# Gated-convolution FFN after pooled attention: VectorE's convolution in units of its middle weight, and three steps moved between engines

## The chip, the cores and the metric

The kernel runs on one core of a Trainium2 chip. The metric is device time in microseconds (us), the median of the runs; a run of the kernel before took 216.84 to 217.48 us. PE is TensorE (matmul), PEld its weight loads, DVE is VectorE, ACT is ScalarE, POOL is GpSimd, SP is the queue that issues most transfers.

## The reference

Inputs are q, k, v of shape (8, 8, 576, 64) in float32 (batch, heads, sequence, head size), and the FFN's weights.

```python
k_p = k.reshape(B, H, Sp, 8, D).mean(axis=3)          # Sp = 72
v_p = v.reshape(B, H, Sp, 8, D).mean(axis=3)
scores = (1 / sqrt(D)) * q @ k_p^T
attn = softmax(scores - max(scores))
x = (attn @ v_p), heads side by side                   # (8, 576, 512)

h = maximum(x @ w_in, 0)                               # (8, 576, 1024)
conv_out[s] = conv_w[0]*h[s-1] + conv_w[1]*h[s] + conv_w[2]*h[s+1]   # per column of h, zero outside
gate = 1 / (1 + exp(-conv_out))
out = (h * gate) @ w_out                               # (8, 576, 512) float32
```

## The kernel before

The eight batches are taken in four groups of two. Attention works on tiles of 128 query rows: ten tiles in group 0 and nine in each later group, 37 in all. For a tile, PE makes the scores of all heads in PSUM (`att_scores`), VectorE takes the maximum of each head (`att_max`, L608) and, from group 1 on, subtracts it (`att_shift`, L620; in group 0 PE adds it), ScalarE takes the exponential (`att_exp`, L646), PE or a transposing DMA turns the result (`att_turn`, `att_send`), PE multiplies by the pooled values (`att_values`, L682), and VectorE divides by the sum of each head: a reciprocal of 8 columns (L695) and a multiplication of 512 columns (L697), both in `att_divide`. The result x is turned into `xT`, by PE in groups 0 and 1 (`att_turn_out`, L714, and a copy), by a DMA on SP's queue in groups 2 and 3 (`att_out`).

The FFN runs per batch, with the hidden columns on the partitions: eight blocks of 128 columns (`fb` 0 to 7), four blocks being a quarter `(b, f4)`, so sixteen quarters in all. PE projects in (`ffn_in`, L727), ScalarE applies Relu into `hT` (`ffn_relu`, L736) with scale 0.5. Then comes the convolution over the sequence, in one of two ways:

- On PE (`ffn_conv`, L889): 64x64 blocks of diagonal matrices `dw`, two blocks `fb` at a time, so that the upper and lower halves of every odd block come out exchanged. ScalarE's tanh (`ffn_tanh`, L914) writes even blocks to `gT` and odd ones to a side buffer `tg`; VectorE adds 1 (`ffn_gate`: L925 for the even blocks, twice L927 for the odd ones, which also puts the halves right) and multiplies by `hT` (`ffn_times`, L935). Ten quarters go this way.
- On VectorE, for the quarters in `Graph.TAPS`, six before: ScalarE makes the middle tap (`ffn_tap`, L862, Identity with a scale per partition) into a float32 buffer of the ring `tg`, which has three, VectorE adds the two side taps (L864), ScalarE takes the tanh (`ffn_tap_tanh`, L869), VectorE adds 1 and multiplies by `hT` (`ffn_tap_gate`, L875 and L876).

The sequence lies in `hT` in nine pieces; for batches in `Graph.WRAP` GpSimd copies 63 columns to each end (`ffn_wrap`, L811, L812), so that each tap is one contiguous read. Since Relu halves h and the weights `convw` are doubled, `tanh(conv / 2) + 1` times `hT` is the gated value.

PE projects out per tile of 128 rows (`ffn_out`, L943), ScalarE or VectorE copies the result (`ffn_copy`, L954), and SP's or ScalarE's queue stores it (`ffn_store`). A tile of the last group needs the gates of all its batches' quarters.

The order of all work is written out: `Graph.ORDER` lists every operation (its index twice, plus one if it takes the second of two engines), `FORMS` the shapes of some matmul groups and `PLACES` the PSUM banks and buffers. Each engine works through its part of that order; a negative entry is a filler matmul. `add(...)` states for each operation its engines, a cost that a planner used, and what it follows.

Of the kernel before, what the change touches and what calls it, by code (L numbers as in the profile page):

```python
# [33 lines left out]
class Graph:  # L34
# [24 lines left out]
    WRAP = (4, 5, 6, 7)  # L59
    TAPS = ((4, 1), (5, 0), (5, 1), (6, 0), (6, 1), (7, 0))  # L60
    ACC = 2
    WRAPS = 2
    CROSS = ()
# [3 lines left out]
    SHIFT_PE = ((0, 0), (0, 1), (0, 2), (0, 3), (0, 4), (0, 5), (0, 6), (0, 7), (0, 8), (0, 9))  # L67
    TURN_DMA = 2
    BANKS = 8
    ORDER = (  # L70
# [107 lines left out]
def kernel(  # L178
# [13 lines left out]
    POOL = 8  # L192
# [1226 lines left out]
```

## Time and profile before

| | |
|---|---|
| runs | 216.84, 217.14, 217.48 us; median 217.14 us |
| the profiled execution | span 216.5 us from the first to the last instruction; no other time of it is given |
| instructions | 6617 |
| mean granted TensorE clock | 0.992 |
| data read, written in HBM | 32.52 MB, 9.44 MB |

A row of the groups gives the line, engine, operation, output and inputs with partitions x columns and type, the count, then busy us in all and the mean ns of one, then the idle time of the engine just before them and what ended it. A row of the stretches gives from:to, the length, and the busy us of PE, PEld, VectorE, ScalarE and GpSimd with their instruction counts, then the granted clock, the busy share of the DMA engines and GB/s. A piece of the chain gives its start, its length and what ran; a row of the timeline the same with shapes, `xN` for a run of N, and in brackets the idle time before it.

### The profile page before, as it was taken

What the parts mean: (1) busy time and instruction counts of PE and PEld (TensorE: products, weight loads), DVE (VectorE), ACT (ScalarE), POOL (GpSimd) and SP (SyncE); (2) the same over time, 40 slices, a digit from 0 to 9 for tenths busy, and PEclk for the clock granted to TensorE, in tenths of its full rate; (3) what the DMA queues carried; (4) which work ended last, traced back from release to release, by engine and by line L of the source; (5) the groups of instructions that cost most, each with busy time, mean ns of one, the idle gap of its engine ahead of it and who ended that gap; (6) DMA issues with size and microseconds to landing.
All of it is one profiled execution on the core that took longest, in us unless ns stands there. A gap on an engine that the chain in (4) does not pass through costs nothing.

```text
span 216.5 us, 6617 instructions
## 1 busy us (share of the span) xinstructions
PE 201.9 (93%) x2753; PEld 137.0 (63%) x2753; DVE 193.2 (89%) x334; ACT 162.7 (75%) x278; POOL 41.5 (19%) x78
## 2 busy tenths in 40 slices
PE   7599999969999999999999899989999999999992
PEld 3557778855788776766776675665656666654451
DVE  7598989999999999999999799999899999998621
ACT  2548885896998887787497594878979999997420
POOL 8644330050052101000000030002201210370000
PEclk9799999999999999999999999999999999999999
DMA  6999999999999999969687634576347745602685
GB/s 210 227 207 209 206 207 208 210 205 206 207 205 206 154 153 179 158 164 165 131 111 100 136 74 89 58 156 148 78 104 153 158 100 123 145 0 51 169 242 171
DMA packets 48833, 33.46 MB, mean 155 GB/s; under 512 B 28300, under 2 KB 43812, under 8 KB 48804
## 3 DMA queue, kind: packets, MB, share of 16 engines
q0 software_dynamic: 15216, 15.40, 43.5%
q1 hardware_dynamic: 32512, 16.13, 36.6%
q10 hardware_dynamic: 1076, 1.52, 2.5%
q8 instruction: 21, 0.34, 0.7%
q14 instruction: 8, 0.07, 0.1%
HBM read 32.52 MB, written 9.44 MB: 194 GB/s over the span
## 4 chain that ended last, share of the span: by engine, by line
PE 45%; DVE 34%; issue 6%; ACT 6%; DMA 5%; SPq 2%; DVEq 0%
PE psum L943 20%; PE psum L727 16%; DVE negm L608 7%; DVE x L697 6%; DVE sd L620 4%; DVE gT L935 4%; DMA hT<-in_k_dram 3%; DVE v L486 3%; DVE gT L927 3%; PE psum L889 2%; DMA out_dram<-osb 2%; DVE r L695 2%; PE psum L682 2%; ACT e L646 2%; DVE gT L925 1%
## 5 line engine op out<-in xcount | busy, mean ns | idle before, releaser
L727 PE MATMUL psum<-xT,w_in_sb 128*128 128x288 bf16 x512 | 74.1, 286 | 2.2 <-DMA xT<-x 1.1
L943 PE MATMUL psum<-w_out_sb,gT 128*128 128x512 bf16 (+1 forms) x296 | 69.5, 374 | 0.7 <-DVE gT L935 0.6
L727 PEld LDWEIGHTS <-w_in_sb 128*128 128x128 bf16 x512 | 47.9, 98 | 19.1 <-issue 2.0
L736 ACT ACTIVATE hT<-psum 128x576 bf16<-128x576 f32 x64 | 40.3, 650 | 14.0 <-PE psum L727 13.4
L943 PEld LDWEIGHTS <-gT 128*128 128x128 bf16 x296 | 27.3, 98 | 26.5 <-issue 0.9
L864 DVE SCALAR_TENSOR_TENSOR tg<-hT,convw,tg 128x576 f32<-128x576 bf16 x48 | 37.6, 815 | 0.5
L608 DVE TENSOR_REDUCE negm<-psum 128x8 f32<-128x576 f32 (+2 forms) x37 | 27.5, 752 | 2.3 <-PE psum L582 1.6
L697 DVE TENSOR_TENSOR x<-psum,r 128x512 bf16<-128x512 f32 (+1 forms) x37 | 25.6, 691 | 1.4
L811 POOL COPY hT<-hT 128x126 bf16<-128x126 bf16 x16 | 7.5, 467 | 97.6 <-ACT hT L736 80.1
L620 DVE TENSOR_TENSOR sd<-psum,negm 128x576 f32<-128x576 f32 x27 | 20.2, 753 | 0.5
L682 PE MATMUL psum<-vm,eT 128*128 128x130 bf16 (+5 forms) x240 | 18.9, 222 | 1.1 <-DVE x L697 0.7
L646 ACT ACTIVATE e<-sd 128x576 bf16<-128x576 f32 x27 | 18.2, 685 | 1.3 <-DVE sd L620 1.1
L954 ACT COPY osb<-psum 128x512 f32<-128x512 f32 x27 | 15.7, 585 | 4.4 <-PE psum L943 4.2
L889 PE MATMUL psum<-hT,dw 64*64 64x288 bf16 (+2 forms) x608 | 18.7, 261 | 0.1
L682 PEld LDWEIGHTS <-eT 128*128 128x128 bf16 (+1 forms) x240 | 15.3, 100 | 5.4 <-DMA eT<-e 1.2
L862 ACT ACTIVATE tg<-hT,convw 128x576 f32<-128x576 bf16 x24 | 18.1, 772 | 0.1
L889 PEld LDWEIGHTS <-dw 64*64 64x64 bf16 x608 | 14.8, 107 | 4.6 <-issue 3.7
L869 ACT ACTIVATE gT<-tg 128x576 bf16<-128x576 f32 x24 | 16.3, 683 | 0.7 <-DVE tg L864 0.5
L914 ACT ACTIVATE gT<-psum 128x576 bf16<-128x576 f32 x20 | 12.9, 651 | 3.9 <-PE psum L889 2.7
L914 ACT ACTIVATE tg<-psum 128x576 bf16<-128x576 f32 x20 | 13.0, 652 | 2.6 <-PE psum L889 1.4
L935 DVE TENSOR_TENSOR gT<-gT,hT 128x2304 bf16<-128x2304 bf16 x10 | 13.5, 1352 | 0.1
L486 DVE TENSOR_TENSOR v<-v 128x1280 bf16<-128x1280 bf16 (+2 forms) x24 | 13.0, 540 | 0.2
(84 smaller groups left out, 234.2 us busy)
## 6 DMA issues: line engine op xcount, KB each, us to landing
out_dram<-osb SPq DMA_DIRECT2D x54, 128.0 KB, 2.4
v<-in_v_dram POOLq DMA_DIRECT2D x8, 512.0 KB, 13.1
qp<-in_q_dram POOLq DMA_DIRECT2D x7, 576.0 KB, 14.4
kk<-in_k_dram POOLq DMA_DIRECT2D x3, 1152.0 KB, 14.6
out_dram<-qp ACTq DMA_DIRECT2D x10, 128.0 KB, 2.7
hT<-in_k_dram SPq DMA_DIRECT2D x2, 576.0 KB, 5.0
w_in_sb<-in_moe_w_in_dram POOLq DMA_DIRECT2D x2, 512.0 KB, 14.2
w_out_sb<-in_moe_w_out_dram POOLq DMA_DIRECT2D x1, 1024.0 KB, 24.7
```

Of the source, the lines that this page charges most:

```text
L608: nc.vector.tensor_reduce(out=a["m"][0:rows], in_=a["s"][0:rows, :, 0:2 * KW].rearrange("p a (h s) -> p a h s", s=Sp), axis=AX.X, op=OP.ma ...
L620: nc.vector.tensor_tensor(out=a["d"][0:rows], in0=a["s"][0:rows, :, 0:2 * KW].rearrange("p a (h s) -> p a h s", s=Sp), in1=a["m"][0:rows]. ...
L646: nc.scalar.activation(out=dst, in_=src, func=ACT.Exp, scale=1.0 / (POOL * 8.0),)
L682: nc.tensor.matmul(out=a["o"][lo:hi, h // 4, (h % 4) * (D + 1):(h % 4 + x1 - x0) * (D + 1)], lhsT=a["eT"][:, j, lo:hi], rhs=buf("vm", b)[: ...
L697: nc.vector.tensor_tensor(out=a["x"][0:rows].rearrange("p (a h d) -> p a h d", a=2, d=D), in0=ov[:, :, :, 0:D], in1=r[0:rows].unsqueeze(3) ...
L727: nc.tensor.matmul(out=banks(ps)[:, j, 0:SC], lhsT=w_in_block(dc, fb), rhs=buf("xT", g)[:, dc, i * S + j * SC:i * S + (j + 1) * SC], start ...
L736: nc.scalar.activation(out=h_of(b)[:, fb].rearrange("p (a s) -> p a s", a=2), in_=banks(ps)[:, :, 0:SC], func=ACT.Relu, scale=0.5,)
L864: nc.vector.scalar_tensor_tensor(out=acc, in0=h, scalar=w, in1=acc, op0=OP.mult, op1=OP.add)
L889: nc.tensor.matmul(out=banks(pss[r ^ c])[c * D:(c + 1) * D, j, lo:hi], lhsT=dw[r * D:(r + 1) * D, tap * n_fb + fb, :], rhs=hT[r * D:(r + 1 ...
L914: nc.scalar.activation(out=t.rearrange("p (a s) -> p a s", a=2), in_=banks(ps)[:, :, 0:SC], func=ACT.Tanh, scale=0.5,)
L935: nc.vector.tensor_tensor(out=gate, in0=gate, in1=h_of(b)[:, four], op=OP.mult)
L943: nc.tensor.matmul(out=bank(ps)[0:rows, columns], lhsT=buf("gT", g)[:, fb, t * P:t * P + rows], rhs=w_out_sb[:, fb, columns], start=(fb == 0),
```

## The change

1. **Taps.** VectorE's convolution is taken in units of the middle weight: `ratio[:, 0]` and `ratio[:, 2]` are the side weights divided by the middle one, `ratio[:, 1]` is half the middle weight, built once by seven small VectorE instructions (a weight of nearly zero is replaced by a tiny one). The first tap reads `hT` twice (`h * ratio + middle h`), the second adds to the buffer, and ScalarE's tanh takes the middle weight as its scale per partition. ScalarE's middle tap goes.
2. **Two more quarters off PE.** (4, 0) and (3, 1) join `TAPS`; batch 3 joins `WRAP`.
3. **Gates cross on ScalarE.** For every quarter left on PE, ScalarE writes an odd block's tanh in two instructions of 64 partitions, each into the exchanged half of `gT`; VectorE then adds 1 in one instruction of 2304 columns in place of three.
4. **Late sigmoids.** In the quarters of batches 6 and 7, ScalarE takes the sigmoid itself (Relu then with scale 1.0), and VectorE's "+1" goes. A sigmoid waits until every exponential has started; the instruction order has one further table load on ScalarE, between the 56th and the 57th Relu.
5. **Split division.** The reciprocal (`att_invert`) and the multiplication (`att_divide`) are operations of their own; the multiplication may go to ScalarE as eight instructions of 64 columns with a scale per partition. The new order puts 9 of 37 there.
6. **The pooling's 1/8 and the scores' 1/8** move from the exponential's scale into the pooling matrix and a scaled identity `ident_k`.
7. `ORDER`, `FORMS` and `PLACES` are new. A form of the exponential by head (`by_head`) is added and not used (`EIGHT = ()`). Output buffers of the last group now follow the turned queries of all of batches 4 to 7.

The changed program's instruction order has, against that of before: on VectorE 64 taps for 48, 12 gate additions for 36, 28 divisions for 37, eight small instructions more in the preparation; on ScalarE 72 division pieces, 48 tanh or sigmoid instructions behind PE's convolution for 40, 32 behind the taps for 24, no middle taps for 24; on PE 480 convolution matmuls for 608 and 26 fillers for 17; on GpSimd 40 edge copies for 32.

```diff
-    WRAP = (4, 5, 6, 7)
-    TAPS = ((4, 1), (5, 0), (5, 1), (6, 0), (6, 1), (7, 0))
+    WRAP = (3, 4, 5, 6, 7)
+    TAPS = ((4, 0), (4, 1), (5, 0), (5, 1), (6, 0), (6, 1), (7, 0), (3, 1))
-    CROSS = ()
+    CROSS = ((0, 0), (0, 1), (1, 0), (1, 1), (2, 0), (2, 1), (3, 0), (3, 1), (4, 0), (4, 1), (5, 0), (5, 1), (6, 0), (6, 1), (7, 0), (7, 1))
+    EIGHT = ()
+    SIG = ((6, 0), (6, 1), (7, 0), (7, 1))
...
+        if part == 3:
+            w, mid, rest = convw.rearrange("p (k f) -> p k f", k=3), ratio[:, 1], ratio[:, 3]
+            nc.vector.tensor_tensor(out=rest, in0=w[:, 1], in1=w[:, 1], op=OP.mult)
+            nc.vector.tensor_scalar(
+                out=rest, in0=rest, scalar1=TINY * TINY, scalar2=2 * TINY, op0=OP.is_lt, op1=OP.mult
+            )
+            nc.vector.tensor_tensor(out=mid, in0=w[:, 1], in1=rest, op=OP.add)
+            nc.vector.reciprocal(out=rest, in_=mid)
+            for k in (0, 2):
+                nc.vector.tensor_tensor(out=ratio[:, k], in0=w[:, k], in1=rest, op=OP.mult)
+            nc.vector.tensor_scalar(out=mid, in0=mid, scalar1=0.5, scalar2=None, op0=OP.mult)
+            return
...
-    def att_divide(g, t):
+    def att_invert(g, t):
+        nc.vector.reciprocal(out=buf("r", g, t)[0:rows_of(g, t)], in_=att_heads(g, t)[:, :, :, D])
+
+    def att_divide(g, t, engine):
...
+        if engine == "ACT":
+            for n in range(H):
+                nc.scalar.activation(
+                    out=a["x"][0:rows, n * D:(n + 1) * D],
+                    in_=ov[:, n // 4, n % 4, 0:D],
+                    func=ACT.Identity,
+                    scale=r[0:rows, n // 4, n % 4:n % 4 + 1],
+                )
+            return
...
-            scale=0.5,
+            scale=1.0 if (b, fb // 4) in Graph.SIG else 0.5,
...
-        if tap == 1:
-            nc.scalar.activation(out=acc, in_=h, func=ACT.Identity, scale=w)
-        else:
-            nc.vector.scalar_tensor_tensor(out=acc, in0=h, scalar=w, in1=acc, op0=OP.mult, op1=OP.add)
+        nc.vector.scalar_tensor_tensor(
+            out=acc, in0=h, scalar=w, in1=acc if tap else mid, op0=OP.mult, op1=OP.add
+        )
+
+    def squash(b, fb):
+        return ACT.Sigmoid if (b, fb // 4) in Graph.SIG else ACT.Tanh
...
-        nc.scalar.activation(out=gate, in_=acc_of(b, fb, ps), func=ACT.Tanh, scale=0.5)
+        nc.scalar.activation(out=gate, in_=acc_of(b, fb, ps), func=squash(b, fb), scale=ratio[:, 1, fb:fb + 1])
...
+            need = tanh
+            if (b, f4) not in Graph.SIG:
+                need = [add(dve(0.78), w, lambda f4=f4: ffn_tap_gate(b, f4), after=tanh, uses=[gtok[g]])]
+            gated = add(dve(1.39), w, lambda f4=f4: ffn_times(b, f4), after=need, uses=[htok[b], gtok[g]])
...
-        o = add(dve(0.2, 0.69), key, lambda: att_divide(g, t), after=[o], uses=[x, rr, big])
+        o = add({"DVE": 0.115}, key, lambda: att_invert(g, t), after=[o], uses=[rr, big])
+        o = add({"DVE": 0.61, "ACT": 0.82}, key, None, after=[o], uses=[x, rr, big])
+        o.emit = lambda o=o: att_divide(g, t, o.engine)
...
+    late = [o for part, o in squashed if part in Graph.SIG]
+    for o in late:
+        for e in exps:
+            e.next.append((o, True))
+            o.left += 1
```

The two-instruction tanh of an odd block in `ffn_tanh` (for quarters in `CROSS`) was in the kernel before and not used.

More of the change, by code (lines that the diff above doesn't have):

```diff
@@ L205 @@
     KP = NJ * P
+    KSCALE = 1.0 / (POOL * 8.0)
+    TINY = 2.0 ** -60
     groups = [[0, 1], [2, 3], [4, 5], [6, 7]]
@@ L224 @@
     ident = const.tile([P, P], BF16, name="ident")
+    ident_k = const.tile([P, P], BF16, name="ident_k")
     mask = const.tile([P, NJ, 3], BF16, name="mask")
@@ L230 @@
     convw = const.tile([P, 3 * n_fb], FP32, name="convw")
+    ratio = const.tile([P, 4, n_fb], FP32, name="ratio")
     ident_2 = const.tile([P, D], BF16, name="ident_2")
@@ L260, with by_head @@
     add = graph.add
+    def by_head(g, t):
+        return (g, t) in Graph.EIGHT
     def shift_by_dve(g, t):
@@ L649, in att_exp @@
             func=ACT.Exp,
-            scale=1.0 / (POOL * 8.0),
         )
@@ L689, in att_values, with att_heads @@
                 )
-    def att_divide(g, t):
+    def att_heads(g, t):
+        return att[g, t]["o"][0:rows_of(g, t), :, 0:4 * (D + 1)].rearrange("p a (h d) -> p a h d", d=D + 1)
+    def att_invert(g, t):
+        nc.vector.reciprocal(out=buf("r", g, t)[0:rows_of(g, t)], in_=att_heads(g, t)[:, :, :, D])
+    def att_divide(g, t, engine):
         a, rows = att[g, t], rows_of(g, t)
-        ov = a["o"][0:rows, :, 0:4 * (D + 1)].rearrange("p a (h d) -> p a h d", d=D + 1)
-        r = buf("r", g, t)
-        nc.vector.reciprocal(out=r[0:rows], in_=ov[:, :, :, D])
+        ov, r = att_heads(g, t), buf("r", g, t)
         a["x"] = buf("x", g, t)
+        if engine == "ACT":
+            for n in range(H):
+                nc.scalar.activation(
+                    out=a["x"][0:rows, n * D:(n + 1) * D],
[3 more added lines that the diff above has]
+                )
+            return
         nc.vector.tensor_tensor(
@@ L905, in ffn_tanh @@
                     in_=banks(ps)[(1 - r) * D:(2 - r) * D, :, 0:SC],
-                    func=ACT.Tanh,
+                    func=squash(b, fb),
                     scale=0.5,
@@ L916, in ffn_tanh @@
             in_=banks(ps)[:, :, 0:SC],
-            func=ACT.Tanh,
+            func=squash(b, fb),
             scale=0.5,
@@ L924, in ffn_gate @@
         gate = gate.rearrange("p (f e) s -> p e f s", e=2)
+        if (b, f4) in Graph.SIG:
+            for r in range(2):
+                nc.vector.tensor_copy(out=gate[r * D:(r + 1) * D, 1], in_=tg[(1 - r) * D:(2 - r) * D])
+            return
         nc.vector.tensor_scalar(out=gate[:, 0], in0=gate[:, 0], scalar1=1.0, scalar2=None, op0=OP.add)
@@ L1074 @@
     dw0 = add({"DVE": 0.3}, soon(), lambda: build_conv_matrices(0, cwtok), after=[cwp], uses=[cwtok])
+    dwr = add({"DVE": 1.2}, START + Graph.DW + 3, lambda: build_conv_matrices(3), after=[dw0])
     dwo = [add({"DVE": 1.0}, START + Graph.DW + n, lambda n=n: build_conv_matrices(n), after=[dw0]) for n in (1, 2)]
@@ L1185 @@
     xtok, xdone = {}, {}
+    exps, squashed = [], []
     def prepared(g, t):
@@ L1209, in add_att @@
         o = add(dve(0.75), key, lambda: att_max(g, t), after=[o], uses=[ng, s])
-        if shift_by_dve(g, t):
+        if by_head(g, t):
+            o = add({"ACT": 0.9}, key, lambda: att_exp(g, t), after=[o], uses=[e, s, ng, lim])
+            exps.append(o)
+        elif shift_by_dve(g, t):
             sd = token("sd", g, t)
@@ L1213, in add_att @@
             o = add(act(0.67), key, lambda: att_exp(g, t), after=[o], uses=[e, sd])
+            exps.append(o)
         else:
@@ L1325, in add_ffn @@
                                                    uses=[cb] + (tg if fb % 2 and tg else [gtok[g]])))
+                squashed.append(((b, f4), tanh[f4][-1]))
             if f2 % 2 and cross:
-                gated = add(dve(0.78, 1.39), w + 6 * f2 + Graph.GATE, lambda f4=f4: ffn_tap_gate(b, f4), after=tanh[f4], uses=[htok[b], gtok[g]])
+                need = tanh[f4]
+                if (b, f4) not in Graph.SIG:
+                    need = [add(dve(0.78), w + 6 * f2 + Graph.GATE, lambda f4=f4: ffn_tap_gate(b, f4), after=tanh[f4], uses=[gtok[g]])]
+                gated = add(dve(1.39), w + 6 * f2 + Graph.GATE, lambda f4=f4: ffn_times(b, f4), after=need, uses=[htok[b], gtok[g]])
                 gdone.setdefault(b, []).append(gated)
@@ L1340, in add_out @@
             key += nudge("ot", 9 * g + t)
-            osb, free = (token("late", g, t), qdone[7, 0]) if g == 3 else (token("osb", g, t), [])
+            osb, free = (token("late", g, t), [x for n in range(4, B) for x in qdone[n, 0]]) if g == 3 else (token("osb", g, t), [])
             need = [a for x in groups[g][0:i + 1] for a in gdone[x]]
```

38 lines of the change are left out of this document (24 added, 14 removed), and 140 rows, old and new, of tables (ORDER, PLACES).

## The prediction

> **What bounds the kernel now.** I read the page's shares first, then busy time by stretch, then the chain that ended last, then the groups and single rows that price the edits. The page's first part, the chain's shares by engine, and the stretches (length, then busy us of PE, PEld, DVE, ACT, POOL, then clock, DMA share and GB/s):
>
> ```profile
> PE 201.9 (93%) x2753; PEld 137.0 (63%) x2753; DVE 193.2 (89%) x334; ACT 162.7 (75%) x278; POOL 41.5 (19%) x78
> ...
> PE 45%; DVE 34%; issue 6%; ACT 6%; DMA 5%; SPq 2%; DVEq 0%
> ```
> ```profile
> 0.00:20.00 20.00, 15.66 (x251) 10.21 (x252) 14.81 (x44) 10.50 (x18) 12.06 (x27) 0.91 1.05 213
> 20.00:119.90 99.90, 95.12 (x1692) 71.52 (x1689) 96.48 (x171) 79.61 (x137) 13.99 (x20) 1.00 1.09 177
> 119.90:203.20 83.30, 82.10 (x766) 50.69 (x767) 79.06 (x117) 70.81 (x120) 15.49 (x32) 1.00 0.49 104
> 203.20:212.30 9.10, 9.05 (x50) 4.61 (x48) 2.38 (x5) 1.75 (x3) 0.00 (x0) 1.00 0.88 249
> ```
>
> From 20 to 119.9 us VectorE is busy 96.48 of 99.90, so its work sets the pace there; PE's 95.12 holds waits inside pipelined matmuls. From 119.9 PE is busy 82.10 of 83.30 and then to 212.3 without a gap, VectorE 79.06 of 83.30, ScalarE 70.81. The cuts stand where these pieces of the chain and of the timeline are:
>
> ```profile
> 119.92 1.15 PE L727 MATMUL psum<-xT,w_in_sb 128*128 128x288 bf16 x8 [1.15 <-DMA xT<-x]
> 201.80 1.36 DVE L935 TENSOR_TENSOR gT<-gT,hT 128x2304 bf16<-128x2304 bf16 x1
> ```
> ```profile
> 82.91 0.74 PE psum L889 x32
> 195.55 0.86 PE psum L889 x24
> 199.10 13.16 PE psum L943 x68
> 212.28 0.42 DVE qp L954
> ```
>
> At 119.92 batch 4's input projection waited for the attention output xT; VectorE's last gate ends at 201.80 + 1.36 = 203.16. Of the 68 last output matmuls 16 are half as wide, so one full one is 13.16 / 60 = 0.22 us. Output tiles 4 to 8 of the last group need that last gate: 32 full and 16 half matmuls, 40 x 0.22 = 8.8 us. So two paths end almost together: VectorE's gates, 203.16 + 8.8 = 212.0, and PE's own queue, 212.26. A gain has to shorten both.
>
> **VectorE, part by part.** The instruction order of the changed program against that of before gives the counts; prices are from these groups, mean ns behind the comma:
>
> ```profile
> L864 DVE SCALAR_TENSOR_TENSOR tg<-hT,convw,tg 128x576 f32<-128x576 bf16 x48 | 37.6, 815 | 0.5
> L697 DVE TENSOR_TENSOR x<-psum,r 128x512 bf16<-128x512 f32 x35 | 24.2, 692 | 1.3
> L927 DVE TENSOR_SCALAR gT<-tg 64x1152 bf16<-64x1152 bf16 x20 | 9.7, 485 | 0.3
> L925 DVE TENSOR_SCALAR gT<-gT 128x1152 bf16<-128x1152 bf16 x10 | 5.4, 542 | 0.0
> L875 DVE TENSOR_SCALAR gT<-gT 128x2304 bf16<-128x2304 bf16 x6 | 4.6, 772 | 0.9 <-ACT gT L869 0.9
> L695 DVE RECIPROCAL r<-psum 128x8 f32<-128x8 f32 x35 | 7.0, 199 | 0.6 <-ACT hT L736 0.6
> L384 DVE TENSOR_SCALAR convw<-psum 128x24 f32<-128x24 f32 x1 | 0.2, 173 | 0.0
> L534 DVE COPY qT<-psum 128x1152 bf16<-128x1152 bf16 x5 | 3.8, 758 | 1.3 <-PE psum L520 1.3
> L534 DVE COPY qT<-psum 128x512 bf16<-128x512 bf16 x1 | 0.4, 425 | 0.1
> L431 DVE CAST kT<-psum 64x144 bf16<-64x144 f32 x2 | 0.6, 312 | 2.6 <-PE psum L406 2.6
> L486 DVE TENSOR_TENSOR v<-v 128x1280 bf16<-128x1280 bf16 x8 | 6.5, 817 | 0.0
> L486 DVE TENSOR_TENSOR v<-v 128x640 bf16<-128x640 bf16 x8 | 3.9, 484 | 0.0
> L486 DVE TENSOR_TENSOR v<-v 128x320 bf16<-128x320 bf16 x8 | 2.6, 319 | 0.1
> L490 DVE TENSOR_TENSOR vm<-v,mask_wide 128x960 bf16<-128x960 bf16 x8 | 5.2, 650 | 0.1
> L954 DVE COPY qp<-psum 128x512 f32<-128x512 f32 x3 | 2.1, 689 | 6.0 <-PE psum L943 6.0
> ```
> ```profile
> 178.09 6.23 DVE L864 SCALAR_TENSOR_TENSOR tg<-hT,convw,tg 128x576 f32<-128x576 bf16 x8
> ```
>
> Eight taps in a row take 6.23 us where 8 x 0.815 would be 6.52, so a queued VectorE instruction costs about 0.05 less than its mean; I take that off each.
> - Taps: 48 become 64, since quarters (3,1) and (4,0) come over. 16 x 0.765 = +12.2. The first tap of a pair now reads a bf16 second source in place of f32, a form that the trace does not show. Its ends are 0.815 and, at the rate of an addition that is bf16 throughout (640 columns in 0.484, L486), 0.45; the output stays f32, so I take 0.815. At 0.45 VectorE would save 11 us more, and PE's path alone would set the end.
> - Gates: the three-piece "+1" of ten quarters goes, -10 x (0.49 + 2 x 0.435) = -13.6; twelve quarters in all (six before) now have the whole-width one, +6 x 0.72 = +4.3; the four sigmoid quarters have none.
> - Division: 9 of 37 go to ScalarE, -9 x 0.64 = -5.8. The reciprocals stay.
> - New small work: seven instructions for the ratios and one for the scaled identity, 8 x about 0.14 (L384, L695) = +1.1.
> - Evacuations change engine: two of q leave (-0.71, -0.38), two key copies (about 0.26 and, twice as wide, 0.4) and one output copy (0.64) come: +0.2.
>
> Sum: 12.2 - 13.6 + 4.3 - 5.8 + 1.1 + 0.2 = -1.6 us. Ahead of the 24th reciprocal, which feeds the transfer that batch 4 waited for, the orders hold: 8 taps more (+6.1), eighteen gate pieces replaced by six whole ones (-8.2 + 4.3), the small work (+1.1), two divisions fewer (-1.3), two q copies fewer (-1.1), two key copies more (+0.7), and one batch's four v steps put behind it (-0.77 - 0.43 - 0.27 - 0.60 = -2.1): -0.5. So batch 4 starts some 0.5 earlier, and the rest, -1.1, falls behind it.
>
> **TensorE.** A convolution pair of (4,0) was 0.86, one of (3,1) 0.74 (chain pieces above, 24 and 32 matmuls): -2 x 0.86 - 2 x 0.74 = -3.2; (3,0) goes from the unwrapped to the wrapped form, +0.24. Behind 119.92 only (4,0) counts fully: -1.7. Nine more filler matmuls stand in the first 20 us, where PE is busy only 15.66: nothing.
>
> **ScalarE.** It loses the middle tap and gets the cross gates, the divisions, a second table load.
>
> ```profile
> L862 ACT ACTIVATE tg<-hT,convw 128x576 f32<-128x576 bf16 x24 | 18.1, 772 | 0.1
> L869 ACT ACTIVATE gT<-tg 128x576 bf16<-128x576 f32 x24 | 16.3, 683 | 0.7 <-DVE tg L864 0.5
> L914 ACT ACTIVATE tg<-psum 128x576 bf16<-128x576 f32 x20 | 13.0, 652 | 2.6 <-PE psum L889 1.4 <-DVE v L486 1.2
> L458 ACT CAST kT<-psum 64x288 bf16<-64x288 f32 x8 | 3.1, 394 | 0.1
> L431 ACT CAST kT<-psum 64x144 bf16<-64x144 f32 x2 | 0.5, 270 | 1.1 <-DVE kT L431 1.1
> L1062 ACT ACT_TABLE_LOAD x1 | 1.3, 1283 | 0.8 <-PEq L1403 0.8
> ```
> ```profile
> 189.86 1.43 ACT L862 ACTIVATE tg<-hT,convw 128x576 f32<-128x576 bf16 x2
> 191.20 1.18 ACT L736 ACTIVATE hT<-psum 128x576 bf16<-128x576 f32 x2
> ```
>
> Two in a row overlap by 0.11 (2 x 0.772 - 1.43). L862 and L869 have the same size and both read SBUF; the one with a scale per partition is 0.09 dearer, and the pair at 1.43 shows that queueing does not hide it. The changed tanh has such a scale.
> - Middle taps: -24 x 0.66 = -15.9. Tanh or sigmoid behind taps: 32 x 0.66 - 24 x 0.57 = +7.4. Cross gates: 48 for 40 instructions, a 64-partition half priced like the whole, +8 x 0.54 = +4.3. Table load +1.3.
> - A division is eight pieces of 64 columns. From 288 to 144 columns a copy falls by 0.124, so 64 columns would be 0.20; less the overlap 0.09; with the scale per partition 0.18; if nothing overlaps, 0.29. I take 0.18, because L862 shows both effects: 1.45 a tile, 9 x 1.45 = +13 (bounds +6.5 and +21).
>
> Together about +10: 162.7 becomes 173. Most of it lies before batch 5, where the cross gates are; from 119.9 on the twenty-odd lost middle taps pay for seven divisions, and 12.5 us of ScalarE's 83.3 were free. So I cost it at nothing; the cover is that idle time.
>
> The new waits: the sigmoids of (6,0) stand behind every exponential (last attention tile), and the tap buffers are three, so VectorE's taps of batch 6 can run only three ahead of them; the order puts gates and divisions there. Divisions on ScalarE queue behind relus, and the xT transfers on SP, with the output stores behind them, wait for them.
>
> **Sum.** VectorE's path: 203.16 - 1.6 + 8.8 = 210.4. PE's path: 212.3 - 0.5 - 1.7 = 210.1. The later one, 210.4 against 212.3, is -1.9, and the way from the last matmul to the end (two narrow copies, stores) stays. The profiled span of 216.5 becomes 214.6. The page gives no other time of that execution; the median of the runs shown, 217.14, is 0.6 above its span, so I forecast 215.2 us.
>
> **Rivals.**
> - *ScalarE's divisions are late (slower).* A tile's x takes 1.45 to 2.3 us on ScalarE for 0.64 on VectorE and waits behind relus. Three of the nine stand within some thirty short instructions behind the 30th of 37 exponentials. For: batch 4 already waited 1.15 us for xT. Against: 12.5 us free. If three in one run reach PE, at 0.8 to 1.7 each, 2.4 to 5.1 us are lost; it ends slower from 1.9 lost on. At 3.8 the time is 217.1 - 1.9 + 3.8 = 219.0, at the low end 217.6. Chance 0.20. The Trainium skill ("ScalarE: Activation LUTs", What ACT_TABLE_LOAD costs) adds a drain of some 1.38 us to a 1.28 us load at each switch of set; L1062 shows the 1283 ns, nothing here shows the drain, and by it ScalarE would lose 1.4 more, and the forecast would be 216.6 if all of that were on the path.
> - *The gain is given back (no change).* VectorE idled only 3.4 us in 20 to 119.9 and 4.2 after (lengths less busy time above); with tap pairs no longer spaced by ScalarE, waits for the three buffers or for GpSimd's edge copies of batch 3 could return the 1.9. Then 217.1. Chance 0.12.
> - *The new order also closes waits (faster still).* If half of VectorE's 7.6 us idle between 20 and 203.2 went, another 3.8 would: 211.4. PE's 1.2 idle after 119.9 speaks against its showing fully. Chance 0.15.
> - That the edits don't do what they say is excluded: the order shows the counts above and one further table load.
>
> **Numbers.** Forecast 0.53. Within 0.3% (0.65 us, about what a measurement of this kernel can tell from no change) lies most of the second rival. Faster: 0.53 + 0.15 + 0.01 = 0.69; same 0.10; slower 0.21. The range goes from the third rival's 211.4, shortened to 211.8 since full effect is unlikely, to 218.3 in the first rival. The forecast's own range, from a quarter of VectorE's idle time saved (-1.9) to one division late (+1.2), is 213.3 to 216.4.
>
> **What would show it.** Right: VectorE's last gate ends near 201.5 and PE's last matmul near 210; taps 64 at 0.77 to 0.82; ScalarE near 173 busy with division pieces at a pitch of 0.18; batch 4's projection starts near 119. Wrong: PE idle of more than 2 us after batch 4 begins with ScalarE's x or xT named; VectorE idle at taps behind tanh; pieces of 0.29 pitch; or a first tap clearly below 0.8.

## The result, and the profile after

The changed kernel takes 228.38 us (median of 4 runs, 226.24 to 229.37) against 217.31 (216.84 to 218.12) for the one before: ratio 1.050, 95% interval 1.044 to 1.056. I had forecast 215.2. The profiled execution took 226.24 us with a span of 224.5; it is the fastest of the four, and what the others lost beyond it no profile shows. Times are of executions in the same state; two of the four runs of e4 below, its profiled one among them, fell in a slower one, and their times are left out.

The page after, its shares by engine and the shares of the chain that ended last:

```profile
PE 200.9 (89%) x2673; PEld 135.6 (60%) x2690; DVE 188.9 (84%) x326; ACT 178.4 (79%) x342; POOL 49.4 (22%) x86
...
PE 54%; ACT 13%; DMA 12%; issue 8%; DVE 5%; POOL 5%; SPq 1%; POOLq 0%; DVEq 0%
```

VectorE and TensorE do less work than before and take longer over it. On the chain VectorE's share falls from 34% to 5%; ScalarE's and the transfers' more than double. The stretches, cut where the prediction cut them (length, busy us of PE, PEld, DVE, ACT, POOL, clock, DMA share, GB/s):

```profile
0.00:20.00 20.00, 15.17 (x228) 9.16 (x229) 15.05 (x48) 9.58 (x16) 10.95 (x26) 1.00 1.01 203
20.00:128.13 108.13, 96.35 (x1689) 72.23 (x1693) 92.84 (x163) 94.36 (x167) 20.00 (x29) 0.97 1.02 165
128.13:211.30 83.17, 80.53 (x712) 49.59 (x722) 78.36 (x113) 72.13 (x155) 18.43 (x32) 1.00 0.55 114
211.30:220.50 9.20, 8.82 (x49) 4.64 (x48) 2.43 (x5) 2.34 (x4) 0.00 (x0) 1.00 0.66 170
```

Batch 4's input projection begins at 128.17 instead of 119.92. From there to the end of the span it is 96.3 us here and 96.6 before, so the whole loss of this execution lies ahead of batch 4: 8.25 us, in a stretch in which VectorE now idles 15.3, TensorE 11.8 (4.8 before), and ScalarE is busy 94.36 of 108.13 (it was 79.61 of 99.90). TensorE's two longest waits there, in the timeline (start, length, engine, and in brackets the wait before it):

```profile
119.31 0.55 PE L716 MATMUL psum<-vm,eT 128*64 128x130 bf16 x12 [2.40 <-DMA eT<-e]
...
128.17 1.63 PE L774 MATMUL psum<-xT,w_in_sb 128*128 128x288 bf16 x12 [1.40 <-DMA xT<-x]
```

The groups that answer to the prediction's prices (busy us, mean ns, then idle time before):

```profile
L910 DVE SCALAR_TENSOR_TENSOR tg<-hT,ratio 128x576 f32<-128x576 bf16 x32 | 25.6, 813 | 1.6 <-ACT gT L920 1.5
L910 DVE SCALAR_TENSOR_TENSOR tg<-hT,ratio,tg 128x576 f32<-128x576 bf16 x32 | 25.0, 812 | 0.1
L925 DVE TENSOR_SCALAR gT<-gT 128x2304 bf16<-128x2304 bf16 x12 | 9.1, 762 | 2.4 <-ACT gT L952 1.5 <-ACT gT L963 0.9
```
```profile
L920 ACT ACTIVATE gT<-tg,ratio 128x576 bf16<-128x576 f32 x32 | 23.9, 783 | 1.8 <-DVE tg L910 1.7
L952 ACT ACTIVATE gT<-psum 64x576 bf16<-64x576 f32 x32 | 20.6, 645 | 2.2 <-PE psum L938 1.8
L737 ACT ACTIVATE x<-psum,r 128x64 bf16<-128x64 f32 x72 | 15.9, 344 | 0.1
L963 ACT ACTIVATE gT<-psum 128x576 bf16<-128x576 f32 x16 | 10.3, 650 | 1.9 <-PE psum L938 1.7
```

### The profile page after: what moved, and what is told of

Same layout as the page of the kernel before. It is cut to its first block, busy times and chain, and to the rows that moved or that the text cites. A ratio compares the mean times of both kernels' runs of the same rounds, so it can differ in the third digit from the quotient of the medians.

```text
span 224.5 us, 6562 instructions
## 1 busy us (share of the span) xinstructions
PE 200.9 (89%) x2673; PEld 135.6 (60%) x2690; DVE 188.9 (84%) x326; ACT 178.4 (79%) x342; POOL 49.4 (22%) x86
## 4 chain that ended last, share of the span: by engine, by line
PE 54%; ACT 13%; DMA 12%; issue 8%; DVE 5%; POOL 5%; SPq 1%; POOLq 0%; DVEq 0%
PE psum L774 19%; PE psum L996 18%; ACT gT L952 6%; PE psum L716 5%; DMA kk<-in_k_dram 5%; PE psum L938 4%; DMA eT<-e 3%; DMA xT<-x 3%; ACT gT L963 3%; POOL hT L859 2%; PE psum L691 1%; DVE negm L632 1%; PE psum L761 1%; PE psum L619 1%; PE psum L544 1%
## 5 line engine op out<-in xcount | busy, mean ns | idle before, releaser
L996 PE MATMUL psum<-w_out_sb,gT 128*128 128x512 bf16 (+1 forms) x279 | 65.7, 373 | 1.5 <-issue 0.3
L774 PEld LDWEIGHTS <-w_in_sb 128*128 128x128 bf16 x512 | 48.5, 98 | 18.3 <-issue 3.2
L910 DVE SCALAR_TENSOR_TENSOR tg<-hT,ratio 128x576 f32<-128x576 bf16 x32 | 25.6, 813 | 1.6 <-ACT gT L920 1.5
L920 ACT ACTIVATE gT<-tg,ratio 128x576 bf16<-128x576 f32 x32 | 23.9, 783 | 1.8 <-DVE tg L910 1.7
L910 DVE SCALAR_TENSOR_TENSOR tg<-hT,ratio,tg 128x576 f32<-128x576 bf16 x32 | 25.0, 812 | 0.1
L716 PE MATMUL psum<-vm,eT 128*128 128x65 bf16 (+5 forms) x240 | 19.2, 222 | 5.7 <-DMA eT<-e 2.9
L952 ACT ACTIVATE gT<-psum 64x576 bf16<-64x576 f32 x32 | 20.6, 645 | 2.2 <-PE psum L938 1.8
L988 DVE TENSOR_TENSOR gT<-gT,hT 128x2304 bf16<-128x2304 bf16 x16 | 21.7, 1361 | 0.2
L744 DVE TENSOR_TENSOR x<-psum,r 128x512 bf16<-128x512 f32 (+1 forms) x28 | 18.8, 682 | 0.4
L938 PE MATMUL psum<-hT,dw 64*64 64x288 bf16 (+1 forms) x480 | 15.8, 270 | 1.3 <-ACT gT L952 0.9
L737 ACT ACTIVATE x<-psum,r 128x64 bf16<-128x64 f32 x72 | 15.9, 344 | 0.1
```

The lines of the kernel that those rows point to most:

```text
L716: nc.tensor.matmul(out=a["o"][lo:hi, h // 4, (h % 4) * (D + 1):(h % 4 + x1 - x0) * (D + 1)], lhsT=a["eT"][:, j, lo:hi], rhs=buf("vm", b)[: ...
L744: nc.vector.tensor_tensor(out=a["x"][0:rows].rearrange("p (a h d) -> p a h d", a=2, d=D), in0=ov[:, :, :, 0:D], in1=r[0:rows].unsqueeze(3) ...
L774: nc.tensor.matmul(out=banks(ps)[:, j, 0:SC], lhsT=w_in_block(dc, fb), rhs=buf("xT", g)[:, dc, i * S + j * SC:i * S + (j + 1) * SC], start ...
L910: nc.vector.scalar_tensor_tensor(out=acc, in0=h, scalar=w, in1=acc if tap else mid, op0=OP.mult, op1=OP.add)
L920: nc.scalar.activation(out=gate, in_=acc_of(b, fb, ps), func=squash(b, fb), scale=ratio[:, 1, fb:fb + 1])
L938: nc.tensor.matmul(out=banks(pss[r ^ c])[c * D:(c + 1) * D, j, lo:hi], lhsT=dw[r * D:(r + 1) * D, tap * n_fb + fb, :], rhs=hT[r * D:(r + 1 ...
```

## The experiments

All runs, with the ratio to the kernel before on the same chip (which took 217.3 to 217.7 us there). "Batch 4" is the start of the 33rd relu in the profiled run, which is the first of batch 4; the 1st, 9th, 17th and 25th begin the four batches ahead of it, and those starts are given in the text where they count.

| run | time, us (range) | ratio, 95% interval | batch 4 |
|---|---|---|---|
| before | 217.31 (216.84 to 218.12) | | 120.6 |
| after | 228.38 (226.24 to 229.37) | 1.050, 1.044 to 1.056 | 128.9 |
| e1 before + cross gates | 226.36 (225.85 to 226.66) | 1.041, 1.035 to 1.046 | 127.0 |
| e2 before + ratio taps | 218.55 (217.99 to 219.77) | 1.005, 1.002 to 1.009 | 121.7 |
| e3 after, 7 quarters uncrossed | 223.55 (222.97 to 225.60) | 1.030, 1.023 to 1.037 | 125.0 |
| e4 after, divisions on VectorE | 230.61 (229.04 to 232.18, two runs) | 1.060, 1.049 to 1.072 | |
| e5 before, straight | 216.09 (215.38 to 216.67) | 0.993, 0.990 to 0.997 | 119.1 |
| e6 before, straight halves | 224.15 (223.54 to 224.22) | 1.029, 1.024 to 1.035 | 125.7 |
| e7 after, straight | 222.95 (222.48 to 224.54) | 1.026, 1.019 to 1.032 | 127.0 |
| e8 e7 + early start | 221.05 (219.50 to 222.52) | 1.016, 1.007 to 1.024 | 124.5 |
| e9 e8 + early q | 220.88 (220.26 to 222.56) | 1.016, 1.010 to 1.021 | 123.2 |
| e10 e9 + early v | 218.82 (217.46 to 220.16) | 1.005, 1.002 to 1.009 | 120.4 |
| e11 before + ratio + sigmoids | 219.45 (218.30 to 221.08) | 1.008, 1.005 to 1.011 | 120.6 |
| e12 after, early start, q and v | 223.64 (222.90 to 224.42) | 1.027, 1.022 to 1.032 | 126.1 |
| e13 e10, nine fillers less | 218.96 (one run) | | 121.2 |
| e14 e12, 6 quarters uncrossed | 220.62 (219.87 to 220.86) | 1.015, 1.009 to 1.021 | 122.4 |

The theories: A, the two half-height tanh of a cross gate are dearer than I had them, and ScalarE is late. B, the new instruction order loses the time in start, loads and transfers. C, the divisions on ScalarE.

**One part at a time (e1 to e4).**

e1, in the kernel before (the edit in short):

```
-            t = buf("tg", b, fb // 4)[:, fb // 2 % 2]      # odd block, one tanh
+            for r in range(2):                             # odd block, two halves crossed
+                gT[r * D:(r + 1) * D, fb] <- tanh(bank[(1 - r) * D:(2 - r) * D])
...
-        gate[:, 0] + 1, then two 64-partition pieces tg + 1
+        gate + 1, whole width
```

> The kernel before, in its own order, with one edit: the tanh of every odd block of its ten convolution quarters is written as two half-height instructions that cross the halves, and the gate has one +1 over the whole width. Theory A (the cross gates cost the time: in the changed kernel a half stands at a pitch of 0.66 us where I had 0.54, and nothing overlaps it, so a pair of blocks takes 2.00 us of ScalarE for 1.08): 20 pairs add about 18 us to ScalarE, which had 20 us free ahead of batch 4; VectorE loses 10 x 0.65 = 6.5 us. ScalarE becomes the late one: 220 to 226 us. Theory B (the new instruction order costs it: loads, transfers and start-up): this kernel keeps the old order, VectorE's saving shows, 213 to 217 us. Theory C (the divisions on ScalarE): as B, none are here.

226.36, just above theory A's range: the cross gates alone, in the old order and with no division moved, cost 8.8 us, although VectorE's busy time fell by 5.3 (193.2 to 187.9). That is theory A. ScalarE in the timeline, two pairs of blocks:

```profile
37.84 0.65 ACT L914 ACTIVATE gT<-psum 128x576 bf16<-128x576 f32 x1 [0.23 <-PE psum L889]
38.52 1.30 ACT L903 ACTIVATE gT<-psum 64x576 bf16<-64x576 f32 x2
39.84 0.65 ACT L914 ACTIVATE gT<-psum 128x576 bf16<-128x576 f32 x1
40.52 1.30 ACT L903 ACTIVATE gT<-psum 64x576 bf16<-64x576 f32 x2
```

From 37.84 to 39.84 a pair takes 2.00 us; every instruction starts when the one ahead has ended (37.84 + 0.65, 38.52 + 1.30).

e2, in the kernel before: `tap == 1` issues nothing, the first tap adds `mid` in place of `acc`, the tanh has `scale=ratio[:, 1, fb:fb + 1]`, and the seven small instructions for the ratios stand at 34.75 us.

> The kernel before, in its own order, with one edit: the convolution on VectorE for its six quarters goes without ScalarE's middle tap, by the ratios of the weights, and the tanh takes the middle weight as its scale. ScalarE loses 24 x 0.66 and pays 24 x 0.09, about 14 us, all of it behind batch 4; VectorE keeps its 48 taps at 0.81 and gets about 1 us of small work early. All theories: batch 4 starts where it did, TensorE's work is the same, so 216 to 218 us; if taps waited for the middle tap, VectorE's last gate ends 1 to 2 us earlier without the end moving, since TensorE's own queue ended with it. If this edit were the loss: over 220.

218.55, 1.0 us over before and 0.6 above the range I gave. In the profiles batch 4 begins 1.0 later (121.7) and the rest is 95.3 us long against 95.9. So the 12.5 us by which ScalarE's busy time fell (162.7 to 150.2) were worth at most 0.6 behind batch 4, which is within the spread of the runs, and the small work on VectorE is the likely cost ahead of it (e11 asks).

e3, in the changed kernel, for seven quarters (in short):

```
-        if fb % 2 and (b, fb // 4) in Graph.CROSS:      # two crossed halves
+        if fb % 2 and (b, fb // 4) in side_of:          # one tanh into a side buffer
...
-        gate + 1, whole width
+        gate[:, 0] + 1, then two 64-partition pieces side + 1
```

The side buffer of quarter (3,0) lies on columns of gT that the output projection of batch 1 still reads, so part of the output is overwritten; the work is the same.

> The changed kernel with the cross gates taken back in the seven convolution quarters ahead of batch 4 (one full-height tanh into a side buffer, three +1 pieces on VectorE); quarter (7,1) keeps them, everything else and the order stay. Theory A: ScalarE loses 14 x 0.93 = 13 us ahead of batch 4, VectorE gets 7 x 0.65 = 4.6 us where it idled about 14; batch 4 begins near 122 to 124 instead of 128.2, and the time is 220 to 224 us. Theory B: the order still loses the time, 227 us or more. Theory C: as B, less than 1 us gained.

223.55: 4.8 us back, as theory A has it, but 6 us over before remain, with 10.6 us of ScalarE's busy time gone (178.4 to 167.8). Theory A is not all.

e4: `att_divide(g, t, "DVE")` for all tiles.

> The changed kernel with all nine ScalarE divisions put on VectorE at their places in the order. ScalarE loses 9 x 1.7 = 15 us, VectorE gets 9 x 0.64 = 5.8. Only two of the nine stand ahead of batch 4. Theory C: batch 4 begins 2 to 3 us earlier and the rest ends earlier too, 222 to 225 us. Theory A: ScalarE gains 3.4 us of the needed 13 ahead of batch 4; 226 to 228 us, or up to 230 where VectorE sets the pace behind it. Theory B: 228 to 230.

230.61, and no run below 229.04: without the divisions on ScalarE the time is no shorter (the changed kernel took 226.24 to 229.37). Theory C falls, and with it the prediction's first rival. Whether these divisions gain anything in this order two runs don't settle.

**The price of a half, and what VectorE's saving is worth (e5, e6).** e5 has one full-height tanh straight into the gate for every block (`t = buf("gT", g)[:, fb, ...]`) and the whole-width +1; e6 has two halves with `in_=banks(ps)[r * D:(r + 1) * D]`. Both leave out the exchange of the halves of an odd block, as e7 to e10 and e13 do below; the amount of work is what is compared.

> The kernel before, in its own order, with the gate of ten convolution quarters as one whole-width +1, and the tanh of an odd block as one full-height instruction straight into the gate. It leaves out the exchange of the two channel halves of the odd blocks. So VectorE gets its saving of 10 x 0.65 = 6.5 us and ScalarE pays nothing. Theory A (the two halves are the price): VectorE was the bound ahead of batch 4, so its seven quarters there let batch 4 begin 2 to 4 us earlier than 120.6, and the time is 212 to 216 us, 11 or more below the crossing kernel's 226.4. Rival D (VectorE did not set the pace ahead of batch 4, loads or TensorE did): 216.5 to 218.

> As the straight kernel, but each odd block's tanh is two half-height instructions, each half onto its own partitions: the exchange is still left out. This asks what keeps two tanh from overlapping. If it is the crossing of partitions (A1), two halves now stand at a pitch of 0.54, a pair of blocks takes 1.62 us, ScalarE pays 20 x 0.54 = 11 us for VectorE's 6.5: 217 to 221. If it is the half height (A2), the pitch stays 0.66 and the time is that of the crossing kernel, 225 to 227.

The timelines of ScalarE, e5 and then e6:

```profile
38.37 2.28 ACT L911 ACTIVATE gT<-psum 128x576 bf16<-128x576 f32 x4 [0.23 <-PE psum L889]
```
```profile
37.87 0.65 ACT L914 ACTIVATE gT<-psum 128x576 bf16<-128x576 f32 x1 [0.23 <-PE psum L889]
38.42 1.29 ACT L903 ACTIVATE gT<-psum 64x576 bf16<-64x576 f32 x2
39.73 0.65 ACT L914 ACTIVATE gT<-psum 128x576 bf16<-128x576 f32 x1
40.28 1.29 ACT L903 ACTIVATE gT<-psum 64x576 bf16<-64x576 f32 x2
```

A pair takes 1.1 us whole (2.28 for two pairs), 1.86 in straight halves, 2.00 crossed. e6's 224.15 lies between the ranges of A1 and A2, and neither holds as I wrote it. In e6 the first half (partitions 0 to 63) starts 0.55 behind the block ahead and overlaps it; the second half (64 to 127) does not overlap the first, nor the next block the second half. In e1 each half has 64 as start of its input or its output, and none overlaps. So what ends the overlap is a change of the start partition, of input or output, from one instruction to the next. Half the height by itself does not: in the kernel before, three 64-partition copies of keys stand in a row, two that read and write partitions 64 to 127 and one on 0 to 63.

```profile
44.83 1.09 ACT L458 CAST kT<-psum 64x288 bf16<-64x288 f32 x3
```

The second starts 0.30 behind the first, ahead of its end (one takes 0.39), the third 0.40 behind the second. The Trainium skill states this rule for VectorE ("VectorE: DVE Perf Modes", Two Vector instructions with no wait between them): an instruction whose input or output starts in another group of 32 partitions than the last one's waits until all before it have finished; the page calls it a model. The pitches here (from one start to the next) agree with it on ScalarE: 0.55 where the starts are equal, 0.65 to 0.68 where one differs.

e5 costs ScalarE nothing, takes 6.2 us from VectorE (193.2 to 187.0), and gains 1.4: rival D more than theory A. Its stretch ahead of batch 4:

```profile
20.00:118.40 98.40, 93.84 (x1684) 71.23 (x1689) 92.13 (x159) 79.65 (x137) 14.03 (x20) 1.00 1.10 180
```

VectorE now idles 6.3 of 98.4 us where it idled 3.4, and the stretch is 1.5 shorter. VectorE had not set the pace by itself.

Who waited for a tanh, in the changed kernel for the halves (L952) and before for the whole ones (L914; us, times):

```profile
  PE psum L716: 1.9, 4
  PE psum L544: 1.6, 2
  DVE gT L925: 1.5, 2
  PE psum L938: 0.9, 1
...
```
```profile
  PE psum L727: 0.6, 2
  PE psum L682: 0.2, 1
```

The halves read PSUM banks that TensorE wants next: values, turned q, the next convolution. That is how they reach TensorE while ScalarE still has idle time elsewhere: in all TensorE waited 5.6 us for halves, and before the change 0.8 for the whole ones.

**The order without the halves' price (e7, e8).** e7 is the changed kernel with e5's edit. e8 moves one entry of ORDER, 12, VectorE's clearing of the pooling matrix:

```
-        0, 10, 24, 16, 4, 44, 28, 8, 36, 12, 14,
+        0, 10, 12, 24, 16, 4, 44, 28, 8, 36, 14,
```

> The changed kernel with the odd blocks' tanh as one full-height instruction straight into the gate (the exchange of the halves is left out), in all eight convolution quarters; the new order, divisions, sigmoids and taps stay. ScalarE loses 16 x 0.93 = 15 us and VectorE pays nothing, so this is cheaper than my forecast had it. Theory A alone: what I forecast, less what I had put on ScalarE for the halves, 212 to 216 us. Theory B (the order, the start and the loads lose time by themselves): 218 to 222, with batch 4 beginning behind 121.

> As the kernel before this one, and VectorE's clearing of the pooling matrix stands ahead of its four clearings of the key buffers again, as in the order before, so that GpSimd builds the matrix and issues the loads behind it about 1.2 us earlier (the key load of batch 1 at 5.74 instead of 6.96). Theory B1 (the load stream, full from 10 to 70 us, sets when a batch can begin): everything behind moves by it, 1.0 to 1.5 us less than without. Rival: the loads have slack, no difference over 0.4 us.

e7: 222.95, a little above B's range, and 6.9 above e5, which has the same tanh in the old order. Theory B holds beside A. e8: 1.9 less (the ranges touch), and in the profile batch 0's first relu goes from 31.58 to 29.45. GpSimd's first microseconds, after and before:

```profile
3.15 1.64 POOL L342 TENSOR_SCALAR_AFFINE_SELECT gT<-gT 64x648 bf16<-64x648 bf16 x2 [1.09 <-DVE gT L353]
...
6.96 0.86 POOL L283 DMA_DIRECT2D kk<-in_k_dram  x1
```
```profile
2.00 1.64 POOL L331 TENSOR_SCALAR_AFFINE_SELECT gT<-gT 64x648 bf16<-64x648 bf16 x2
...
5.74 0.81 POOL L272 DMA_DIRECT2D kk<-in_k_dram  x1
```

In the new order VectorE clears four key buffers ahead of the pooling matrix, GpSimd waits 1.09 for it, and every load behind it goes out 1.2 later.

**Two late loads (e9, e10, e12).** In the changed kernel batch 7's v is loaded at 104.39, before at 80.70 (GpSimd's queue):

```profile
104.39 0.74 POOL L316 DMA_DIRECT2D v<-in_v_dram  x1 [5.32 <-DVE vm L514]
```
```profile
80.70 0.77 POOL L305 DMA_DIRECT2D v<-in_v_dram  x1 [5.27 <-DVE vm L490]
```

And SyncE's transfer that turns batch 7's q takes 6.96 us at 105.59, before 2.03 at 98.43; behind it in the queue stand the transfers of xT and eT that TensorE waits for:

```profile
105.59 6.96 SPq L552 DMA_TRANSPOSE qT<-qp  x1
112.64 1.22 SPq L753 DMA_TRANSPOSE xT<-x  x1
113.95 1.18 SPq L1019 DMA_DIRECT2D out_dram<-osb  x2
115.24 3.44 SPq L700 DMA_TRANSPOSE eT<-e  x2
```
```profile
98.43 2.03 SPq L528 DMA_TRANSPOSE qT<-qp  x1
```

e9 moves batch 7's q (entry 98) ahead of the key pair (92). e10 also moves batch 5's last v step (176) behind its third, gives that step value buffer 3, and moves batch 7's v (100) behind batch 6's. e12 is the changed kernel, cross gates and all, with these moves and e8's.

> The straight kernel with the earlier start, and one load moved: batch 7's q is issued ahead of the key pair of batches 6 and 7 on GpSimd's queue (near 62 to 64 us instead of 82.5), as in the order before; its buffer has been free since batch 1. The exchange of the halves is left out as before. What is to be told apart is why SyncE's transfer that turns this q takes 6.9 us instead of 2.0 and TensorE then waits for eT and xT between 104 and 124. Theory Q (the transfer waits for its own load): it falls to 2 to 3 us, TensorE's idle time there shrinks by 3 to 4, 217 to 218.5 us. Theory V (the load of batch 7's v, issued at 100.6 instead of 80.7, runs into it): the transfer stays at 6 to 7 us, 220.5 to 221.5.

> As the kernel before this one, and also batch 5's last v step stands right behind its third again (in a value buffer of its own, so that it waits for nobody), and batch 7's v is issued right behind batch 6's, ahead of batch 3's edge copies. Its load then goes out near 78 to 81 us, as before the change. Theory V: SyncE's transfer of q falls to 2 to 3 us only here; TensorE waits 3 to 4 us less for eT and xT, 216.5 to 218.5 us. Theory Q: no more than 0.5 below the kernel before this one. If neither moves it, the waits between 104 and 124 come from the order of the transfers on SyncE's queue itself: 220 to 221.5.

> The changed kernel itself, cross gates and all, with the earlier start and the early loads of q and v for batch 7: only its order is mended. Theory A: the cross gates still hold TensorE up by 5 to 6 us ahead of batch 4; the start gives 1 to 2 us, the loads what they gave to the straight kernel: 222 to 226. Rival: once ScalarE is late, start and loads hide behind it, no more than 1 us is won: 227 to 228.5.

The same transfer in e9 and in e10:

```profile
100.32 6.51 SPq L556 DMA_TRANSPOSE qT<-qp  x1
```
```profile
100.92 3.27 SPq L556 DMA_TRANSPOSE qT<-qp  x1
```

Theory V: an earlier q changes neither the transfer nor the time (220.88); with v's load at 82.35 the transfer takes 3.27 and the time falls by 2.1 to 218.82 (V's range ended at 218.5), and batch 4 begins at 120.4, as before the change. In the changed kernel itself (e12) start and loads together are worth 4.7 us, and the transfer there takes 3.45.

**What is left (e11, e13, e14).** e11 is e2 with the ratios on GpSimd (but for the reciprocal) and sigmoids without the +1 for batches 6 and 7.

> The kernel before, in its own order, with the two parts of the change that cost ScalarE nothing: the ratio convolution for its six quarters (the ratios built on GpSimd but for one reciprocal, so that VectorE pays 0.2 us early instead of 1.2), and sigmoids without the +1 for batches 6 and 7 (four +1 steps of VectorE go; in this order, too, they stand behind every exponential). If the 1.0 us that the ratio alone lost ahead of batch 4 was its small work on VectorE, batch 4 begins where it did before, and the tail keeps the 0.6 us that the ratio won: 216.4 to 217.2. VectorE's last gate ends 2 to 4 us earlier, but TensorE's own queue bounds the tail, so no more than 1 us comes of it. If the loss had another cause: 218 to 219.

Batch 4 begins at 120.6, so the 1.0 us of e2 was the small work on VectorE; but the time is 219.45, above both ranges. The profiled execution was among that run's fastest (218.45, span 216.7), and TensorE's longest waits in it are much those of before, so why the median is higher stays open. None of the runs with the reference's full computation beats the kernel before.

e13 leaves out nine fillers. The question is this stop of TensorE, which e10 has at 49.06 and e3, e4, e7, e8, e9, e12 and e14 have at the same matmul:

```profile
49.06 0.22 PE L623 MATMUL psum<-kT,qT 128*128 128x144 bf16 x1 [3.07 <-issue]
```

> The straight kernel with early start and loads, less nine of the filler matmuls of the first 20 us (18 instructions of TensorE's stream). It asks what the 3.1 us are in which TensorE stands at the fourth matmul of one score tile near 46 to 49 us with no wait of the program and none that the profile shows; in five kernels that share this order it is the same matmul. Theory F (the instruction itself arrives late, at a fixed place of the stream): the stop moves 18 instructions on, to the last matmul of the transposes of e behind it. Rival (a wait on data or a buffer that the profile does not show): it stays at the fourth score matmul. Time within 1 us of 218.8 in either.

```profile
45.91 0.66 PE L550 MATMUL psum<-ident,qp 64*64 64x64 bf16 x56 [1.22 <-issue]
...
48.64 0.69 PE L625 MATMUL psum<-kT,qT 128*128 128x144 bf16 x4
49.12 0.63 PE L767 MATMUL psum<-ident,x 128*128 128x128 bf16 x4
49.54 0.63 PE L697 MATMUL psum<-ident,e 128*128 128x128 bf16 x4
52.11 0.22 PE L697 MATMUL psum<-ident,e 128*128 128x128 bf16 x1 [1.93 <-issue]
```

The four score matmuls run through, and the stop stands at the fifth transpose of e, 18 instructions on. Theory F: the instruction arrives late at a fixed place of TensorE's stream, its 864th matmul in all nine kernels. e13 stops a second time, at 45.91, at its 736th: 128 matmuls and as many weight loads earlier. The traces also hold the transfers of the DMA queue that the page lists as "instruction" (q8, 21 transfers of 16 KB). In e10 one of them runs from 46.79 to 47.76, and TensorE goes on at 49.06; in all ten stops TensorE goes on 1.26 to 1.48 us behind the end of such a transfer. So it waited for its instructions. The Trainium skill ("Runtime: NRT & Kernel Launch", Instruction fetch mechanics) has instructions fetched in blocks of 256 by a DMA queue and the cost mostly hidden; the distance of e13's two stops agrees with the 256, and 3.07 us is not hidden. What made the transfer late was not tried. In the changed kernel, TensorE came to this place so late that it waited only 0.38 there: the stop shows when the halves' delay is gone.

TensorE's granted clock is the second thing that the profiles of the new order share. In the changed kernel it is 0.50 from 48.5 to 51.9 and from 120.2 to 123.6, both ahead of batch 4; in e10 from 50.2 to 53.6. Before the change it is 1.00 from 20 to 212.3. In e10, six output matmuls at the half clock take as long as twelve behind it:

```profile
50.98 2.75 PE L987 MATMUL psum<-w_out_sb,gT 128*128 128x512 bf16 x6 [0.22 <-issue]
...
54.42 2.75 PE L987 MATMUL psum<-w_out_sb,gT 128*128 128x512 bf16 x12
```

By that, 3.4 us at half the clock cost TensorE up to 1.7 us (an estimate). Every profile of the new order has such a stretch, beginning between 47.0 and 53.9; no profile of the old order has one between 20 us and its last 3. The ten runs of e10 go with it: the six with a mean clock under 0.985 took 218.23 to 220.16, the four above 217.46 to 218.64. No run tries what brings it about.

> The changed kernel with all three repairs and the reference's result: early start, early loads, and the cross gates taken back in six of the seven convolution quarters ahead of batch 4 (full-height tanh, three +1 pieces on VectorE). If the three losses are the whole of what the change cost above its own gains, it lands where the straight kernel did plus what VectorE's pieces and the two crossed quarters left bring back: 219 to 221 us, 1 to 2% slower than before. If order and gates had gained what I forecast once the losses are gone: 215 to 217.

220.62: with start and loads mended, the cross gates taken back in six of the seven quarters, and the full computation, the change is still 1.5% slower than before. No gain of its own shows.

## Why the prediction was wrong, step by step

Of the 13.2 us between 215.2 and 228.38, start and loads are 4.7 (after less e12), the halves 4.8 (e12 less e10, whose tanh cost nothing, as I had charged them), and 3.6 are left (e10 less the forecast). Taken in the other order the same medians give 5.4 for the halves (after less e7) and 4.1 for start and loads (e7 less e10), so each part is known to about 1 us.

- *Taps and first tap: right.* 0.813 and 0.812 against 0.815. VectorE's work fell by 4.3, more than the 1.6 forecast; it did not matter.
- *"VectorE is busy 96.48 of 99.90, so its work sets the pace there": wrong.* e5 took 6.2 us from it and gained 1.4. TensorE at 95.12 was as close, and I set it aside. So a gain on VectorE shows there only in part.
- *ScalarE, "cross gates +8 x 0.54 = +4.3": mis-sized.* By pitch, 20 pairs at 1.08 before are 21.6 us, and 16 pairs at 2.00 after are 32.0: +10.4. I priced a half like a whole at its overlapped pitch; it has no overlap. ScalarE's sum came to +15.7 instead of +10. The division pieces took 0.22 each (15.9 / 72) instead of 0.18, inside the bounds. The second table load took its 1283 ns at 185.79, and the next tanh began 0.56 behind its end; of the drain that the prediction mentions no more than that can show.
- *"So I cost it at nothing; the cover is that idle time": the step that failed.* I found the idle time behind batch 4 and the cross gates ahead of it. There ScalarE had 20 us free, but not between a convolution and the matmul that wants its banks. e1, which has nothing but the cross gates, is 8.8 slower; in the changed kernel they are worth 4.8.
- *"One batch's four v steps put behind it: -2.1": a cost counted as a gain.* What waited for those steps was not VectorE's but GpSimd's queue: batch 7's v load went from 80.70 to 104.39 and into SyncE's transfer. I did not follow the moved step to the load that its buffer holds back.
- *"Nine more fillers: nothing."* The fillers show no cost (218.96 without nine of them, one run, against 218.82), but the four clearings moved ahead of the pooling matrix in the same lines cost 1.2 to 1.9, and I did not list them.
- *Batch 4 "some 0.5 earlier": 8.25 later.* All of the above, with TensorE at half its clock for twice 3.4 us on the way.
- *TensorE behind batch 4, -1.7: right in work, lost in waits.* Over the 92.5 us from batch 4's start, the sums of the stretches, before and then after:

```profile
sum 92.50, PE 91.14 PEld 55.30 DVE 81.55 ACT 72.56 POOL 15.49; mean PE 15.19 PEld 9.22 DVE 13.59 ACT 12.09 POOL 2.58
```
```profile
sum 92.50, PE 89.34 PEld 54.23 DVE 80.92 ACT 74.48 POOL 18.43; mean PE 14.89 PEld 9.04 DVE 13.49 ACT 12.41 POOL 3.07
```

TensorE has 1.8 less to do and idles 3.2 instead of 1.4; the way to the end stays. That is the second rival's outcome for that stretch; of the causes it named, the wait for a tap buffer shows (1.5 us of VectorE, L910 behind L920 above).
- *First rival, divisions late:* named ScalarE's lateness, but by the wrong work; e4 shows that without them the time is no shorter.

What would prove it wrong was partly named: TensorE idle with xT as the cause did show (1.40), as batch 4 began rather than behind it, and VectorE did idle at taps behind a tanh. The 3.6 us are not fully split. e10 is 2.7 above e5, which has the same tanh in the old order; TensorE's stop at 49 (3.07 in e10), its half clock behind it and e2's 1.0 lie in that, and what each is worth by itself was not tried.

## What to carry to other kernels

Price an instruction on part of the partitions by rows of such instructions, neighbours included: four 64-partition copies on ScalarE, of 0.394 each by their group, stood in the timeline before the change without any overlap (they alternate between the two halves), and I had not asked:

```profile
74.19 1.61 ACT L458 CAST kT<-psum 64x288 bf16<-64x288 f32 x4
```

Where two engines are both above 95% busy, neither can be called the bound until one is relieved by itself; e5, a small edit, would have settled it. And follow every moved step to the buffer it frees, the load that waits for that buffer, and the queue that the load then meets.

## What the runs showed that I had not expected

- On ScalarE two neighbours overlap, by about 0.11 us, only where input and output start at the same partitions: a tanh of 576 columns follows the last one after 0.55 us, and after 0.65 to 0.68 where a start differs (e5, e6, e1).
- The DMA transpose of batch 7's q held SyncE's queue for 2.03 to 3.45 us with no load issued beside it, and for 6.27 to 6.96 with one of 512 KB issued 0.8 to 1.7 us ahead; all behind it in the queue moved by that.
- TensorE stopped for 1.2 to 3.2 us at fixed places of its instruction stream, with no wait of the program, and went on 1.26 to 1.48 us behind a transfer of the instruction queue; with 18 instructions less in front the place moved by 18.
- TensorE's granted clock fell to 0.50 for 3.4 us near 50 us in every profile of the new order (6.8 in e8), behind idle time of TensorE such as the 3.07 us in e10; but not every idle stretch is followed by it (the 1.15 us until 119.92 before the change are not).
